# A decode-attention kernel's first weight load, issued as 16 rows and then 112

## The chip, the cores and the metric

The kernel runs on one core of a Trainium2 chip. The metric is device time in microseconds (us) of one execution, with all inputs in HBM. The median of three runs is compared.

## The reference, cut to what matters

Two independent attention blocks, A and B, each with its own inputs, are computed and joined along the last axis. Each is one decode step for 8 sequences with 32 heads of 128 and a cache of 4096 positions, in bfloat16:

```python
B, Sq, D = 8, 1, 1024
H, Sk, Dh = 32, 4096, 128
...
q = (lambda x, *d: x.transpose(*d))((x @ wq).reshape(B, Sq, H, Dh), 0, 2, 1, 3)
scores = jnp.einsum("bhqd,bhkd->bhqk", q, k_cache) * (Dh ** -0.5)
p = _softmax(scores, axis=-1)
o = jnp.einsum("bhqk,bhkd->bhqd", p, v_cache)
return (lambda x, *d: x.transpose(*d))(o, 0, 2, 1, 3).reshape(B, Sq, H * Dh) @ wo
```

The caches are 8 x 32 x 4096 x 128 each. With the four of them, the two `wq` and the two `wo`, the core reads 1107 MB in all.

## The kernel before, in words

The work is cut into 64 tiles (`NQ`), each for one sequence of one block and 8 of its heads. A tile's keys are 8 MiB in SBUF: 128 partitions of 64 KB. Partition `u*16 + m` holds head `u` and the `m`-th sixteenth of the positions. A tile's values have the same shape, and so do a `wq` and a `wo`.

All of these go through one buffer, `ring`, with three slots of 128 partitions x 64 KB. A list named `plan` fixes the order of the loads and the slot of each: `wq` of A into slot 1, the first keys into slot 0, `wq` of B into slot 2, and then keys and values in turn. `load_tiles` walks along that list. It issues a load as soon as the instruction that last reads the slot's former tenant is known, and makes the load wait for that instruction. Every load is one DMA on SyncE's queue (SP), issued at line 208 of the helper `dma`. A DMA adds 16 to a semaphore when it has landed; there is one semaphore for each slot (`("t", w)`), and `_Program` counts what each reader has to wait for.

The instructions of every engine are written into lists first (`P.add`) and then emitted. SyncE's list is emitted in two parts: its first two instructions, the loads of `wq` of A and of the first keys, stand ahead of the block in which all engines start (`part=(0, 2)`), the rest inside it (`part=(2, None)`). The repeated middle of the other engines' lists is emitted as loops whose waits grow by a fixed step.

At the start the small input `x` of both blocks is loaded on ScalarE's queue into the first 8 partitions of slot 2 (16 KB for each block). TensorE transposes it (line 447) into `xT`; then slot 2 is free for `wq` of B. `make_q` (line 285) multiplies `xT` with `wq`, `make_qT` (line 301) transposes the queries, and `make_stage` and `make_qbc` (lines 312 to 319) copy the query of a tile to all partitions that need it.

For each tile, in four chunks, VectorE multiplies the keys with the query in place (line 330) and folds the result once (line 335); TensorE sums it further through an identity (line 345), and VectorE finishes the sum (line 353). After the four chunks VectorE and ScalarE make the softmax (lines 359 to 365), VectorE spreads the weights (line 370), and TensorE multiplies them with the values (line 382). The last matmuls at line 345 free a key slot, those at line 382 a value slot. At the end `make_proj` (line 431) multiplies with `wo`, whose last load is cut into four along its columns, and two DMAs write the result.

Of the kernel before, what the change touches and what calls it, by code (L numbers as in the profile page):

```python
# [31 lines left out]
class _Program:  # L32
# [11 lines left out]
    def add(self, eng, emit, deps=(), dma_key=None, moves=False):  # L44
        op = _Op(eng, emit, list(deps), dma_key, moves)
        if dma_key is not None:
            self.counts[dma_key] = self.counts.get(dma_key, 0) + 16
            op.token = (dma_key, self.counts[dma_key])
        for d in op.deps:
            if not (d.eng == "pe" and eng == "pe"):  # L50
                d.sig = True
        self.ops[eng].append(op)
        return op
# [86 lines left out]
def _build_kernel(nc, caches, out):  # L140
    B, Sq, D = caches[0][0].shape
    _, H, Sk, Dh = caches[0][1].shape
    NC = len(caches)
    assert B == 8 and Sq == 1 and Dh == 128 and Sk == 4096 and D == 1024 and H % 8 == 0 and 128 % H == 0
    DC = D // 128
# [16 lines left out]
    with es:  # L162
# [36 lines left out]
        sems = {e: es.enter_context(nc.semaphore(f"c_{e}")) for e in ENGINES[1:]}  # L199
# [4 lines left out]
        P = _Program()  # L204
        add = P.add

        def dma(out_ap, in_ap, key, deps, eng="sp"):
            return add(eng, lambda e: e.dma_start(out_ap, in_ap), deps, dma_key=key)
# [22 lines left out]
        opT, opMul, opEacc, opRed, opNgm, opExp = {}, {}, {}, {}, {}, {}  # L231
# [18 lines left out]
        def where(n):  # L250

            return n // (B * HB), n // HB % B, n % HB
# [4 lines left out]
        def load_tiles():  # L257
            while issued[0] < len(plan):
                kind, n, w = plan[issued[0]]
                prev = before[issued[0]]  # L260
                dep = opUse.get(prev)
                if prev is not None and dep is None:
                    return
                to, key = ring[:, w, :], ("t", w)
                if kind in ("k", "v"):
                    c, b, hb = where(n)
                    from_ = caches[c][1 if kind == "k" else 2][b, hb * HQ:(hb + 1) * HQ].rearrange("u (m t) d -> (u m) (t d)", m=MP)
                    opT[(kind, n)] = dma(to, from_, key, [dep])
                elif kind == "wq":
                    opT[(kind, n)] = dma(to[:, 0:DC * H * Dh], caches[n][3].rearrange("(p k) n -> p (k n)", k=DC), key, [dep])  # L270
                else:
                    from_ = caches[n][4].rearrange("(p r) n -> p (r n)", r=H)
                    for i, (r0, r1) in enumerate(wo_cuts if n == NC - 1 else ((0, H),)):
                        opT[(kind, n, i)] = dma(to[:, r0 * D:r1 * D], from_[:, r0 * D:r1 * D], key if n < NC - 1 else ("w", i), [dep])
                issued[0] += 1
# [167 lines left out]
        def emit_xT(e):  # L443
# [5 lines left out]
            return i  # L449
        op_xT = opUse[("x", 0)] = add("pe", emit_xT, [c_ident, op_x[-1]])  # L450
        load_tiles()
        c_xT = add("dve", lambda e: e.tensor_copy(xT[:], misc_bf16[:, 0:NC * DC * B]), [op_xT])
        make_q(0)
# [5 lines left out]
        for n in range(NQ):  # L459
            P.mark(n)  # L460
            for r in range(NR):
                s = n * NR + r
                make_mul(s)
                if s >= LAG:
                    make_red(s - LAG)
                if r == LAG - 1 and n >= 1:
                    make_shift(n - 1)
                fold = make_fold(s)
                if r == LAG - 1 and n >= 1:
                    make_pm(n - 1)  # L470
                if n == 0 and r == NR - 1:
                    for c in range(1, NC):
                        make_q(c)
                        make_qT(c)
                if r == 2 and n >= 1:
                    make_pv(n - 1, 0, RG // 2)
                if r == 3 and n >= 1:
                    make_pv(n - 1, RG // 2, RG)
                    make_acc(n - 1)
                if r == 2 and n + 1 < NQ:  # L480
                    make_stage(n + 1)
                    make_qbc(n + 1)
                make_eacc(s, fold)
                load_tiles()
                if r == 3 and n >= 1:
                    make_ext(n - 1)
        P.mark(NQ)
        n = NQ - 1
# [4 lines left out]
        make_pv(n, 0, RG)  # L493
        make_acc(n)
        load_tiles()
        make_ext(n)
        make_norm(1)
# [6 lines left out]
            o.token = (("x", 0), 16 * NC)  # L504
        loops = {"pe": (1, 2, (NQ - 2) // 2), "dve": (3, 2, (NQ - 4) // 2), "act": (3, HB, (NQ - 4) // HB)}

        P.run("sp", nc.sync, sems, part=(0, 2))
        with nc.Block() as block:

            @block.sync  # L510
            def _(eng):
                P.run("sp", eng, sems, part=(2, None))

            @block.tensor
            def _(eng):
                P.run("pe", eng, sems, loops["pe"])

            @block.scalar
            def _(eng):
                P.run("act", eng, sems, loops["act"])  # L520

            @block.vector
            def _(eng):
                P.run("dve", eng, sems, loops["dve"])

            @block.gpsimd
            def _(eng):
                P.run("pool", eng, sems)
# [4 lines left out]
def bass_concat_heads__mha_block_cached__mha_block_cached__decode_kernel(  # L533
    nc, A_x, A_k_cache, A_v_cache, A_wq, A_wo, B_x, B_k_cache, B_v_cache, B_wq, B_wo, out,
):
    caches = [(A_x, A_k_cache, A_v_cache, A_wq, A_wo), (B_x, B_k_cache, B_v_cache, B_wq, B_wo)]
    _build_kernel(nc, caches, out)
# [28 lines left out]
```

## Time and profile before

| | |
|---|---|
| runs | 2563.64, 2563.65, 2563.33 us (median 2563.64) |
| profiled execution, span from the first to the last instruction | 2562.3 us; the median of the runs lies 1.3 us above it |
| busy share of the span | VectorE 85%, TensorE 44%, ScalarE 5%, GpSimd 0% |
| DMA | 1107.51 MB in 19554 packets, mean 432 GB/s |
| mean granted TensorE clock | 0.685 |

Times of a profile are microseconds from the start of its span. PE is TensorE, PEld its weight loads, DVE VectorE, ACT ScalarE, POOL GpSimd; SPq and ACTq are the queues on which SyncE and ScalarE issue DMAs. A row of a timeline is: start, duration, engine, line, operation, what is written and read, the count, and in brackets how long the engine had been idle and what ended that. A row of a window is: the stretch and its length, the busy time and the number of instructions of PE, PEld, DVE, ACT and POOL, the granted clock, the mean busy share of the 16 DMA engines, and the GB/s. A packet's bytes and time are counted in the window in which it starts, so a short window can show a share above 1.

### The profile page before, as it was taken

How to read it: one execution, taken by the hardware profiler on the slowest of the kernel's cores; microseconds unless marked ns; L12 is line 12 of the kernel's file. 1: busy time of each engine (PE TensorE's matmuls, PEld its weight loads, DVE VectorE, ACT ScalarE, POOL GpSimd, SP SyncE). 2: the span in 40 equal slices, each digit the busy share in tenths (PEclk: the TensorE clock that was granted, in tenths of full speed). 3: DMA queues.
4: the chain of work that ended last, by engine and by line, in shares of the span. 5: the costliest groups of instructions: out<-in, count | busy, mean ns of one | idle time of the engine just before them, and what ended most of it. 6: DMA issues, size and time to landing. Idle time of an engine off the chain costs nothing.

```text
span 2562.3 us, 18832 instructions
## 1 busy us (share of the span) xinstructions
PE 1115.7 (44%) x7712; PEld 396.7 (15%) x7712; DVE 2170.6 (85%) x1042; ACT 129.9 (5%) x401; POOL 2.6 (0%) x15
## 2 busy tenths in 40 slices
PE   2443443443443443444444444434444434434434
PEld 1111111111111111111111111111111111111112
DVE  3898898898898898898898888988988988988983
ACT  1100000000000000000000000000000000000000
POOL 0000000000000000000000000000000000000000
PEclk7676766767767767766666766767667666767667
DMA  9999999999999999999999999999999999999999
GB/s 425 427 438 430 437 431 436 432 436 432 435 431 437 430 438 430 435 432 435 433 431 437 431 435 433 434 433 435 433 435 433 435 433 435 433 435 433 435 433 394
DMA packets 19554, 1107.51 MB, mean 432 GB/s; under 512 B 2184, under 2 KB 2248, under 8 KB 2520
## 3 DMA queue, kind: packets, MB, share of 16 engines
q1 hardware_dynamic: 19512, 1107.34, 99.9%
q8 instruction: 7, 0.11, 0.0%
q10 hardware_dynamic: 32, 0.03, 0.0%
q14 instruction: 3, 0.02, 0.0%
HBM read 1107.33 MB, written 0.03 MB: 432 GB/s over the span
## 4 chain that ended last, share of the span: by engine, by line
DMA 52%; DVE 28%; issue 16%; PE 4%; ACT 0%; another core or an unknown queue 0%; DVEq 0%; SPq 0%
DMA ring<-in_A_k_cache_dram 25%; DMA ring<-in_B_k_cache_dram 25%; DVE ring L330 10%; DVE ring L335 10%; PE red L345 4%; DVE s_sb L353 4%; DVE PM L370 3%; DMA ring<-in_B_wo_dram 2%; DVE rmax L359 1%; DVE rtmp L360 0%; ACT PM L291 0%; DVEq L135 0%; DVE ngm L363 0%; PE o L285 0%
## 5 line engine op out<-in xcount | busy, mean ns | idle before, releaser
L330 DVE TENSOR_TENSOR ring<-ring,qbc 128x8192 bf16<-128x8192 bf16 x256 | 1131.7, 4421 | 310.9 <-DMA ring<-in_A_k_cache_dram 158.0
L345 PE MATMUL red<-ring,ident 128*128 128x512 bf16 x2048 | 780.1, 550 | 1392.7 <-DVE ring L335 1392.7
L335 DVE TENSOR_TENSOR ring<-ring 128x4096 bf16<-128x4096 bf16 x256 | 582.3, 2274 | 0.0
L345 PEld LDWEIGHTS red<-ring,ident 128*128 128x128 bf16 x2048 | 238.5, 127 | 1842.6 <-DVE ring L335 1495.2
L353 DVE TENSOR_REDUCE s_sb<-red 128x64 f32<-128x1024 f32 x256 | 312.0, 1219 | 2.9 <-PE red L345 2.9
L382 PE MATMUL pv<-ring,PM 128*32 128x512 bf16 x4096 | 274.4, 415 | 4.6 <-DVE PM L370 4.6
L370 DVE TENSOR_TENSOR PM<-pe,own_h 128x2048 bf16<-128x2048 bf16 x64 | 146.2, 2284 | 0.7 <-ACT pe L365 0.7
L382 PEld LDWEIGHTS pv<-ring,PM 128*32 128x32 bf16 x4096 | 103.9, 104 | 188.4 <-issue 116.2
L319 ACT ACTIVATE qbc<-misc 128x128 bf16<-128x128 f32 x64 | 17.8, 278 | 1093.4 <-PE misc L317 1093.4
L365 ACT ACTIVATE pe<-s_sb,ngm 128x256 bf16<-128x256 f32 x64 | 32.5, 508 | 470.2 <-DVE ngm L363 470.2
L390 ACT ACTIVATE accS<-pv 128x512 bf16<-128x512 f32 x64 | 38.2, 597 | 350.5 <-PE pv L382 350.5
L399 PEld LDWEIGHTS o<-accS,E 128*32 128x32 bf16 x1024 | 31.3, 100 | 49.3 <-issue 48.1
L399 PE MATMUL o<-accS,E 128*32 128x32 bf16 x1024 | 38.1, 185 | 0.7 <-ACT accS L390 0.7
L405 ACT ACTIVATE o_sb<-o 32x32 f32 (+1 forms) x64 | 11.9, 186 | 449.5 <-PE o L399 448.9
L359 DVE TENSOR_REDUCE rmax<-s_sb 128x1 f32<-128x256 f32 x64 | 26.9, 420 | 2.2
L435 DVE CAST orow<-proj 128x256 bf16<-128x256 f32 x2 | 0.8, 424 | 28.7 <-PE proj L431 28.7
L431 PE MATMUL proj<-ring,on_sb 128*32 128x256 bf16 x256 | 12.1, 363 | 17.7 <-DMA ring<-in_A_wo_dram 9.9
L312 ACT ACTIVATE qst<-qT 128x128 bf16 (+1 forms) x64 | 18.7, 293 | 2.0 <-DVE qT L305 2.0
L305 DVE COPY qT<-misc 128x64 bf16<-128x64 bf16 x8 | 3.5, 436 | 17.6 <-PE misc L301 17.6
L360 DVE TENSOR_SCALAR rtmp<-half,rmax 128x32 f32<-128x32 f32 x64 | 15.4, 241 | 2.2
L363 DVE TRANSPOSE_TENSOR_REDUCE ngm<-rtmp 128x1 f32<-128x32 f32 x64 | 13.5, 211 | 2.2
L317 PE MATMUL misc<-ident,qst 128*128 128x128 bf16 x64 | 14.8, 232 | 0.9 <-ACT qst L312 0.9
(33 smaller groups left out, 65.5 us busy)
## 6 DMA issues: line engine op xcount, KB each, us to landing
ring<-in_B_wo_dram SPq DMA_DIRECT2D x1, 5120.0 KB, 33.6
ring<-in_B_wo_dram SPq DMA_DIRECT2D x1, 2048.0 KB, 38.2
ring<-in_B_wo_dram SPq DMA_DIRECT2D x1, 768.0 KB, 39.6
ring<-in_A_k_cache_dram SPq DMA_DIRECT2D x32, 40.0
ring<-in_A_v_cache_dram SPq DMA_DIRECT2D x32, 27.8
ring<-in_B_k_cache_dram SPq DMA_DIRECT2D x32, 39.8
ring<-in_B_v_cache_dram SPq DMA_DIRECT2D x32, 27.8
ring<-in_B_wo_dram SPq DMA_DIRECT2D x1, 256.0 KB, 39.7
```

Of the source, the lines that this page charges most:

```text
L312: return e.activation(qst[:, n % 2, :].rearrange("p (j m) -> p j m", m=MP), from_.unsqueeze(2).to_broadcast([128, HQ, MP]), ACTF.Copy)
L319: opQbc[n] = add("act", lambda e: e.activation(qbc[:, n % 2, :], misc[:, 0:Dh], ACTF.Copy), [opQb[n], _at(opMul, NR * (n - 2) + NR - 1)])
L330: opMul[s] = add("dve", lambda e: e.tensor_tensor(v, v, qbc[:, n % 2, :].unsqueeze(1).to_broadcast([128, CT, Dh]), ALU.mult), [opT[("k", n ...
L335: return add("dve", lambda e: e.tensor_tensor(v[:, :, 0:64], v[:, :, 0:64], v[:, :, 64:128], ALU.add), [opMul[s]])
L345: i = e.matmul(dst, ident[:], v[:, g, :, j, :], start=(j == 0), stop=(j == 3))
L353: opRed[s] = add("dve", lambda e: e.tensor_reduce(s_sb[:, n % 2, r * CT:(r + 1) * CT], red_ps[s % 2][:, :].rearrange("p (t w) -> p t w", w ...
L359: m = add("dve", lambda e: e.tensor_reduce(rmax[:], s_sb[:, n % 2, :], AX.X, ALU.max), [opRed[NR * n + NR - 1]])
L365: opExp[n] = add("act", lambda e, at: e.activation(pe[:], s_sb[:, n % 2, :], ACTF.Exp, bias=ngm[:, n % 2:n % 2 + 1], scale=scale, accum_ou ...
L370: opPM[n] = add("dve", lambda e: e.tensor_tensor(PM[:], pe[:].unsqueeze(2).to_broadcast([128, T, HQ]), own_h[:].unsqueeze(1).to_broadcast( ...
L382: i = e.matmul(pv_ps[32 * q:32 * (q + 1), :], PM[:, t:t + 4, :].rearrange("p t j -> p (t j)"), v[:, t * Dh:(t + 4) * Dh], start=(g == 0), ...
L390: opAcc[n] = add("act", lambda e: e.activation(accS[:], pv_ps[:], ACTF.Copy), [opPV[n], _at(opExt, n - 1)])
L399: x = e.matmul(to, E[:, i, PH - 1 - u:PH - 1 - u + MB], accS[:, i * 128 + H * u:i * 128 + H * (u + 1)], start=(i == 0 and u == 0), stop=(i ...
```

## The change

The first load of the list, `wq` of block A, is issued as two DMAs one after the other on the same queue: the first takes partitions 0 to 15, the second partitions 16 to 127. Both add to the semaphore of slot 1, and the readers wait for both. `wq` of B stays one DMA. Since SyncE's list is one instruction longer at its head, three instead of two of its instructions are emitted ahead of the block, so the first keys' load still is. Nothing else is changed.

```diff
                 elif kind == "wq":
-                    opT[(kind, n)] = dma(to[:, 0:DC * H * Dh], caches[n][3].rearrange("(p k) n -> p (k n)", k=DC), key, [dep])
+                    from_ = caches[n][3].rearrange("(p k) n -> p (k n)", k=DC)
+                    for p0, p1 in ((0, 16), (16, 128)) if n == 0 else ((0, 128),):
+                        opT[(kind, n)] = dma(to[p0:p1, 0:DC * H * Dh], from_[p0:p1, :], key, [dep])
...
-        P.run("sp", nc.sync, sems, part=(0, 2))
+        P.run("sp", nc.sync, sems, part=(0, 3))
...
-                P.run("sp", eng, sems, part=(2, None))
+                P.run("sp", eng, sems, part=(3, None))
```

## The prediction

> **What bounds the kernel now.** I read the page's head first, then its queues, then the windows of the steady part, then the issues and the chain of the first 60 us, and last the first five microseconds in narrow windows.
>
> ```profile
> span 2562.3 us, 18832 instructions
> DMA  9999999999999999999999999999999999999999
> GB/s 425 427 438 430 437 431 436 432 436 432 435 431 437 430 438 430 435 432 435 433 431 437 431 435 433 434 433 435 433 435 433 435 433 435 433 435 433 435 433 394
> q1 hardware_dynamic: 19512, 1107.34, 99.9%
> DMA 52%; DVE 28%; issue 16%; PE 4%; ACT 0%; another core or an unknown queue 0%; DVEq 0%; SPq 0%
> ```
>
> ```profile
> 0.00:80.00 80.00, 27.35 (x241) 11.15 (x242) 33.84 (x23) 11.76 (x21) 2.60 (x15) 0.76 0.98 421
> 80.00:2480.00 2400.00, 1051.89 (x6992) 366.66 (x6990) 2096.48 (x992) 115.17 (x371) 0.00 (x0) 0.68 1.00 434
> 2480.00:2562.30 82.30, 36.44 (x482) 18.91 (x480) 40.23 (x27) 2.95 (x9) 0.00 (x0) 0.67 0.94 403
> ```
>
> The last two columns of the windows are the DMA engines' mean busy share and the GB/s. From 80 to 2480 us the sixteen engines are busy all the time (1.00) at 434 GB/s, and VectorE, the busiest compute engine, has 2096 of 2400 us. SyncE's queue q1 alone takes 99.9% of the engines' span. So the engines that move the caches set the time, and there is no idle stretch in which a delay of theirs could be made up: what the first load loses or gains comes out at the end, nearly one for one. One engine moves 434 / 16 = 27.1 GB/s, so a ring row of 64 KB costs it 2.42 us, and a whole load of 128 rows (8.39 MB) 19.3 us.
>
> ```profile
> 0.80 0.39 SPq L208 DMA_DIRECT2D ring<-in_A_wq_dram  x1
> 1.26 0.41 SPq L208 DMA_DIRECT2D ring<-in_A_k_cache_dram  x1
> 16.89 0.33 SPq L208 DMA_DIRECT2D ring<-in_B_wq_dram  x1
> 29.25 0.33 SPq L208 DMA_DIRECT2D ring<-in_A_k_cache_dram  x1
> ...
> ring<-in_A_wq_dram SPq DMA_DIRECT2D x1, 22.1
> ...
> 23.03 3.59 PE L285 MATMUL o<-ring,xT 128*8 128x512 bf16 x32 [6.17 <-DMA ring<-in_A_wq_dram]
> ...
> 34.33 0.28 ACT L319 ACTIVATE qbc<-misc 128x128 bf16<-128x128 f32 x1 [0.38 <-PE misc L317]
> ...
> 43.48 4.43 DVE L330 TENSOR_TENSOR ring<-ring,qbc 128x8192 bf16<-128x8192 bf16 x1 [9.87 <-DMA ring<-in_A_k_cache_dram]
> ```
>
> These are the starts of the DMAs on SyncE's queue and of the compute that waits for them. The load to be split is issued at 0.80 and lands 22.1 us later; the first key tile is right behind it in the same queue, and VectorE waits for that tile until 43.48. The queries' side work (23.03 to 34.6) ends 9 us before that, so what sets VectorE's start is the transfers.
>
> **The change part by part.** It splits one issue of 128 rows into one of rows 0 to 15 and one of rows 16 to 127, in the same queue and ahead of everything else. The bytes are the same; no compute instruction is changed. What the sixteen engines do at the start today is seen in narrow windows; a window counts a transfer's bytes where the transfer starts.
>
> ```profile
> 0.00:1.75 1.75, 0.00 (x0) 0.00 (x0) 0.00 (x0) 0.00 (x0) 0.86 (x8) 1.00 0.00 0
> 1.75:1.85 0.10, 0.00 (x0) 0.00 (x0) 0.00 (x0) 0.00 (x0) 0.10 (x1) 1.00 6.00 1966
> 1.85:1.95 0.10, 0.00 (x0) 0.00 (x0) 0.00 (x0) 0.00 (x0) 0.07 (x1) 1.00 9.74 3277
> 1.95:2.05 0.10, 0.00 (x0) 0.00 (x0) 0.00 (x0) 0.00 (x0) 0.06 (x1) 1.00 10.00 3277
> 2.05:2.15 0.10, 0.00 (x0) 0.00 (x0) 0.00 (x0) 0.00 (x0) 0.10 (x1) 1.00 4.03 1311
> 2.15:2.70 0.55, 0.00 (x0) 0.00 (x0) 0.38 (x3) 0.00 (x0) 0.41 (x3) 1.00 0.28 119
> 2.70:4.80 2.10, 0.00 (x0) 0.00 (x0) 0.03 (x1) 1.28 (x1) 1.01 (x5) 1.00 0.00 0
> 4.80:5.40 0.60, 0.00 (x0) 0.00 (x0) 0.00 (x0) 0.00 (x0) 0.00 (x0) 1.00 4.03 1748
> ```
>
> GB/s times microseconds gives KB: 197 + 328 + 328 + 131 + 65 = 1049 KB, which is 16 rows of 65.5 KB. Then nothing starts for 2.1 us, and between 4.80 and 5.40 the next 1049 KB start. So the undivided load already begins with a wave of 16 rows, one for each engine, of which 15 start within 0.4 us. All that is left to gain lies ahead of it.
>
> *The earlier start, a gain.* From the issue at 0.80 to the first rows (1.75 to 1.85) pass about 1.0 us, and the last engine starts in 2.15 to 2.70. If a short load came out of the queue faster, the stagger of 15 engines (0.4 us) and some of the 1.0 us could go. Bounds: 0 and 1.0 us; I take 0.2, since the SyncE issue of a full load (0.33 to 0.41 us) is the only part of that wait that can plainly depend on the number of rows. [...]
>
> *One issue more on SyncE.* 0.33 to 0.41 us by the rows above. It moves the first key load from 1.26 to about 1.7, which is needed when the engines run out of the first load, about 21 us: hidden under 19 us of transfers. The 112 rows are issued at about 1.2 and are needed at 4.80, when the first wave ends; if that cover of 3 us were gone, the 0.4 us would show. Everything further down that queue waits for compute (16.89, 29.25) and not for SyncE. The ScalarE queue's x loads share the engines row by row; if they come later, the transposes and the issue at 16.89 come later too, but the engines have the first key tile to move until about 41 us, so 24 us hide that. Cost: 0.
>
> *The wait.* Both parts count on the same semaphore and the matmuls at 23.03 wait for both; every later count on it is 16 higher. No wait instruction is added. Cost: 0.
>
> *The narrow destination, the price.* Today 16 rows are in flight at a time as well, but as parts of a transfer over all 128 rows of the ring. In the change the first wave goes to 16 neighbouring rows of SBUF. No load of the trace is like that, so I bound it. Lower end: the engines set the pace and the wave costs 2.42 us as any other, extra 0. Upper end: the write side takes a rate in proportion to the rows that a transfer spans. The row of 434 GB/s for 128 then gives 54 GB/s for 16, and 1049 KB take 19.4 us, extra 16.9. Neither end has a nearer row than the other; I take the middle, 10.9 us for the wave, extra 8.5. [...]
>
> *The 112 rows.* They make seven rows for each engine instead of eight. 128 rows are evidently dealt out so that the engines don't hinder each other (434 GB/s); 112 rows that begin at row 16 are another deal, and neighbours may share what 128 rows keep apart. Lower end: 7 x 2.42 = 16.9 us, extra 0. Upper end: the slowest engine meets another's rows at each of its seven, each costs one more row time, extra 16.9. I take two of seven, 4.8 us, nearer to the lower end because the full load, the closest in kind, shows no such loss. The slowest engine counts, since a load has landed only when its last row has, and at share 1.00 that engine has no pause in which to catch up.
>
> Sum: -0.2 + 0 + 0 + 8.5 + 4.8 = +13.1 us. The profiled execution's span of 2562.3 becomes 2575.4; the median of the three runs, 2563.64, stands 1.3 above that span, so the forecast is 2576.7 us, 0.5% slower. A measurement of this kernel can tell about 0.2%, or 5.1 us, from no change.
>
> **The rivals.** *Nothing to see.* The write side has room for sixteen engines on any rows, or rows are dealt to the engines by their address, so that the split changes no engine's list. Then only the start moves, by -1.0 to +0.4: about 2563.4 us, not slower. For it: the first wave today is 16 rows at once and the rate drops in none of the 40 slices but the last; the decisive point is whether the first wave of 16 rows ends at 4.80 to 5.40 as now. Against it: all of those loads span 128 rows, so they say nothing of 16 neighbours.
>
> *The whole first load crowded.* If the 112 rows are dealt to the engines like cards, each wave of sixteen goes to neighbouring rows, and all eight waves pay 8.5 us: +68, 2631 us. For it: a wave is one row for each engine, and if neighbouring rows go to the engines in turn in the first, they may in the other seven. Against: a full load then should suffer too, and it runs at 434 GB/s.
>
> *A faster start that carries through.* The gain's upper bound is 1.0 us, 0.04%, so it stays below what can be told; to be faster by 5.1 us the whole startup of 1.8 us would not be enough.
>
> **How the numbers follow.** Forecast (crowded first wave, some crowding behind it, from +5.1 to +19) 0.67; nothing to see 0.24; the whole load crowded 0.08; a gain over 5.1 us 0.01. So faster 0.01, same 0.24, slower 0.75. The forecast's own range is 2568.7 to 2582.6, its top being 16.9 for the first wave and a little of the second part. The range has to leave out no more than 2 in 10: with the likeliest case alone it would leave out 3, so it reaches down over "nothing to see" to 2563.0, and the wholly crowded load stays outside: 2563.0 to 2582.6.
>
> **What would show it.** In the first five microseconds the first wave of 1049 KB should start about as now, and the next rows not at 4.80 but near 13. The landing of the first load, as seen by the first L285 matmul, moves from 23.03 to about 36, the first L330 from 43.48 to about 56.6. The first slice of GB/s (a fortieth, 64 us) falls from 425 to about 425 x (64 - 13) / 64 = 338, while the DMA share stays at 9 because crowded engines count as busy; from 80 us on every slice keeps its rate, and the end lies 13 us later. The step of the narrow destination is wrong if the second wave starts by 5.4; the step of the 112 rows is wrong if the landing's delay equals the first wave's; the step of no recovery is wrong if the first L330 is late by more than the end is.

## The result, and the profile after

The changed kernel takes 2585.38 us (median of 5 runs, 2584.42 to 2585.89), the one before 2563.43 (5 runs): a ratio of 1.0085, interval 1.0074 to 1.0096, or 22.0 us more. The forecast was 2576.7, in a range up to 2582.6. The direction was right and so was the place where the time goes, the first load; the size was not.

The page of the changed kernel, its span, the 40 slices and the queue:

```profile
span 2584.6 us, 18863 instructions
DMA  9999999999999999999999999999999999999998
GB/s 288 426 435 435 428 435 436 435 429 436 434 428 436 436 434 429 437 434 428 435 436 432 432 436 433 430 435 435 431 434 435 434 430 435 435 431 434 435 434 385
q1 hardware_dynamic: 19528, 1107.34, 99.8%
```

The first slice falls from 425 to 288 GB/s, and from the second on the rate is what it was. The DMA share stays at 9 in that slice, though only two thirds of the bytes move (288 against 425 GB/s): the share counts an engine as busy while a row takes it longer, and the first 16 rows take 8.6 us each on average (5.94 x 1.45 in the second window below). The GB/s show the loss, the share hides it.

The starts of the first transfers, in windows:

```profile
0.00:1.75 1.75, 0.00 (x0) 0.00 (x0) 0.00 (x0) 0.00 (x0) 0.86 (x8) 1.00 0.00 0
1.75:3.20 1.45, 0.00 (x0) 0.00 (x0) 0.41 (x3) 0.00 (x0) 1.09 (x5) 1.00 5.94 723
3.20:10.00 6.80, 0.00 (x0) 0.00 (x0) 0.00 (x0) 1.28 (x1) 0.66 (x4) 1.00 0.06 10
10.00:11.70 1.70, 0.00 (x0) 0.00 (x0) 0.00 (x0) 0.00 (x0) 0.00 (x0) 1.00 3.08 578
11.70:22.00 10.30, 0.00 (x0) 0.00 (x0) 0.00 (x0) 0.00 (x0) 0.00 (x0) 1.00 0.79 205
22.00:45.30 23.30, 1.12 (x17) 1.09 (x18) 0.23 (x1) 0.00 (x0) 0.00 (x0) 1.00 0.98 259
45.30:80.00 34.70, 11.03 (x105) 4.14 (x105) 15.87 (x9) 5.50 (x11) 0.00 (x0) 0.66 0.99 427
```

The first wave of 16 rows (1.45 x 723 = 1048 KB) starts as before. Of the second wave, which started between 4.80 and 5.40 before, a single row (6.80 x 10 = 68 KB) starts before 10 us, and the other 15 (983 KB) between 10 and 11.7. So the first wave ran some 5.5 us longer. But the rate stays low behind it too, at 205 and 259 GB/s, until the load has landed near 45. So the first piece isn't the only slow part: 5.5 of the 22 us show in its wave, and the rest behind it, in the 112 rows.

The timeline of the changed kernel (lines are two higher than before):

```profile
0.80 0.87 SPq L208 DMA_DIRECT2D ring<-in_A_wq_dram  x2
1.71 0.43 SPq L208 DMA_DIRECT2D ring<-in_A_k_cache_dram  x1
...
30.00 1.11 PE L449 MATMUL misc<-ident,ring 8*128 8x8 bf16 x16 [30.00 <-DMA ring<-in_B_x_dram]
31.14 0.35 SPq L208 DMA_DIRECT2D ring<-in_B_wq_dram  x1
...
45.30 3.58 PE L287 MATMUL o<-ring,xT 128*8 128x512 bf16 x32 [14.19 <-DMA ring<-in_A_wq_dram]
...
65.84 4.42 DVE L332 TENSOR_TENSOR ring<-ring,qbc 128x8192 bf16<-128x8192 bf16 x1 [10.10 <-DMA ring<-in_A_k_cache_dram]
```

The first matmul on the load is 22.3 us later (23.03 before), VectorE's first multiplication 22.4 us (43.48), and the span is 22.3 us longer. Nothing is given back in the 2500 us between.

### The profile page after: what moved, and what is told of

It reads as the page before. It is cut to its first block, busy times and chain, and to the rows that moved or that the text cites. A ratio compares the mean times of both kernels' runs of the same rounds, so it can differ in the third digit from the quotient of the medians.

```text
span 2584.6 us, 18863 instructions
## 1 busy us (share of the span) xinstructions
PE 1121.7 (43%) x7712; PEld 398.3 (15%) x7712; DVE 2170.6 (84%) x1042; ACT 130.0 (5%) x401; POOL 2.6 (0%) x15
## 4 chain that ended last, share of the span: by engine, by line
DMA 51%; DVE 27%; issue 17%; PE 4%; another core or an unknown queue 1%; ACT 0%; DVEq 0%; SPq 0%
DMA ring<-in_B_k_cache_dram 25%; DMA ring<-in_A_k_cache_dram 23%; DVE ring L332 10%; DVE ring L337 10%; PE red L347 4%; DVE PM L372 3%; DVE s_sb L355 2%; DMA ring<-in_A_wq_dram 2%; DMA ring<-in_B_wo_dram 2%; DVE rmax L361 1%; DVE rtmp L362 0%; ACT PM L293 0%; PE o L287 0%; DVEq L135 0%
```

## The experiments

Four theories were held against each other. *Ports*, as the expectations call it: where the rows lie in SBUF decides. The name was the author's assumption; no run shows what lies behind the place. *Span*, the prediction's upper bound: the rate follows the number of rows that a transfer spans. *Read side*: neighbouring source rows in HBM crowd. *Issue*: the second DMA itself costs. Each run changes the one load only, and where it needs it the number of SyncE's instructions ahead of the block; only112 also fills the rows that it doesn't load, and splitB cuts the load of B in place of A's. The diffs are shortened to the loop over the pieces of the load in question. Times are medians, with the ratio and its interval; the kernel before took 2563.4 to 2563.5 us beside them.

**Cut along the columns instead of the rows (cols).**

```diff
-for p0, p1 in ((0, 16), (16, 128)): dma(to[p0:p1, 0:DC * H * Dh], from_[p0:p1, :], key, [dep])
+for c0, c1 in ((0, 4096), (4096, DC * H * Dh)): dma(to[:, c0:c1], from_[:, c0:c1], key, [dep])
```

> The first load in two DMAs again, but both of 128 rows: columns 0 to 4095 (8 KB of every row, 1 MiB as in the change) and then the other 56 KB. Four theories stand. Ports: the place of the rows in SBUF sets the rate, so nothing is lost here, 2563.4 us within 1. Span: the rate follows the number of rows that a transfer spans, so nothing is lost either. Read side: the source rows are those of before, nothing lost. Issue: a second DMA on the queue with its 16 completions is what costs; then this one is at 2585 as the change is.

Measured: 2563.35 us, ratio 1.000 (0.999 to 1.0009). Two issues, two completions and 1 MiB first cost nothing. *Issue* is out, and a first piece of 1 MiB gains nothing either.

**Eight DMAs of 16 neighbours (nb16), and of every eighth row (st8).**

```diff
+for q in range(8): dma(to[16 * q:16 * q + 16, 0:DC * H * Dh], from_[16 * q:16 * q + 16, :], key, [dep])   # nb16
+for q in range(8): dma(to[q:128:8, 0:DC * H * Dh], from_[q:128:8, :], key, [dep])                         # st8
```

> The first load in eight DMAs of 16 neighbouring rows each. Ports: each of the eight waves is like the first of the change, which lasted from 1.8 to about 10 us, 8.2 us or 5.3 to 5.8 more than a wave of before; +42 to +46, about 2607 us. [...] Span: 16.9 us more for each wave, +135, 2698. Read side: as ports. Issue: seven more issues at 22 us, +154.

> The first load in eight DMAs of 16 rows each, every eighth row (0, 8, 16, ... and so on). [...] Span: each wave spans all 128 rows, +0, 2563. Read side, if neighbouring source rows are what crowds: the source rows are eight apart, +0, 2563. Issue: +154.

Measured: 2618.64 (ratio 1.0215, 1.0198 to 1.0232) and 2584.80 (1.0083, 1.0066 to 1.01). Per wave the extra is 55.1 / 8 = 6.9 us and 21.3 / 8 = 2.66 us. A wave of 16 neighbours takes 2.42 + 6.9 = 9.3 us, 113 GB/s, and one of every eighth row 5.1 us, 206 GB/s: 3.8 and 2.1 times as long as 2.42. *Span* is out: every eighth row spans the whole buffer and still loses half the rate (206 GB/s of 434).

**The 112 rows written out as blocks of seven (blk7).**

```diff
+for p0, p1, ps in ((0, 16, 1), *((16 + i, 122 + i, 7) for i in range(7))): dma(to[p0:p1:ps, 0:DC * H * Dh], from_[p0:p1:ps, :], key, [dep])
```

> The change with its 112 rows written out as seven DMAs of 16 rows, row 16 + i + 7e for engine e. If the one DMA of 112 rows is dealt to the engines in blocks of seven neighbouring rows, this has the same waves as the change and its time: 2585.4 within 2 us, with the first matmul on the load near 45.3. If the 112 rows are dealt otherwise, the waves behind the first differ: with rows in turn they would be those of the run of 16 neighbours, and blocks written out would come out well under 2585. Issue: six more issues, far above 2600.

Measured: 2585.27 (1.0085, 1.0068 to 1.0102), the changed kernel's time to 0.1 us. The total alone proves little, since every eighth row gave 2584.8 too. The windows say more. Between 20.5 and 22 us 16 rows start in the changed kernel and in this run, in this order below, and none in the third line, which is of the halves further down:

```profile
20.50:22.00 1.50, 0.00 (x0) 0.00 (x0) 0.00 (x0) 0.00 (x0) 0.00 (x0) 1.00 2.18 699
20.50:22.00 1.50, 0.00 (x0) 0.00 (x0) 0.00 (x0) 0.00 (x0) 0.00 (x0) 1.00 2.20 709
20.50:22.00 1.50, 0.00 (x0) 0.00 (x0) 0.00 (x0) 0.00 (x0) 0.00 (x0) 1.00 0.00 0
```

So a DMA of 112 rows behaves as seven DMAs of rows 16 + i + 7e do: as if each engine had seven neighbouring rows. Had each engine every sixteenth row, all waves would be those of the run of 16 neighbours.

**Every second row of 32 (st2), and source and destination exchanged (nb_from_st8, st8_from_nb).**

```diff
+for q in range(8): rows = slice(32 * (q // 2) + q % 2, 32 * (q // 2) + 32, 2); dma(to[rows, 0:DC * H * Dh], from_[rows, :], key, [dep])   # st2
+for q in range(8): dma(to[16 * q:16 * q + 16, 0:DC * H * Dh], from_[q:128:8, :], key, [dep])                         # nb_from_st8
+for q in range(8): dma(to[q:128:8, 0:DC * H * Dh], from_[16 * q:16 * q + 16, :], key, [dep])                         # st8_from_nb
```

> The first load in eight DMAs of 16 rows each, every second row of a group of 32. [...] Span: each wave spans a quarter of the rows, 109 GB/s, 9.7 us a wave, +58, 2621, and far from the run with every eighth row. Read side: between the neighbours and every eighth row.

> Eight DMAs of 16 rows: the destination rows are 16 neighbours, the source rows every eighth (so wq of A stands in SBUF with its rows permuted, and the queries of A are other ones; the work and the bytes are the same). Ports or span: as the run of 16 neighbours in both, about 2607 or what that run gave. Read side: as the run with every eighth row in both.

> Eight DMAs of 16 rows: the destination rows are every eighth, the source rows 16 neighbours (wq of A with its rows permuted; the same work and bytes). [...] Read side: as the run of 16 neighbours in both, about 2607 or more.

Measured: 2584.99, 2618.37 and 2584.64 us (ratios 1.0084, 1.0067 to 1.0101; 1.0215, 1.0198 to 1.0232; 1.0082, 1.0065 to 1.0099). Rows spread over 32 cost what rows spread over 128 cost, against *span* again. With the source exchanged nothing moves: to 16 neighbours it is 2618.4 whatever is read, to every eighth row 2584.6. *Read side* is out for these two patterns, and the destination alone decides. For the 112 rows, whose source rows lie seven apart, the two sides were not exchanged.

**The 112 rows alone (only112).**

```diff
-for p0, p1 in ((0, 16), (16, 128)):
+for p0, p1 in ((16, 128),):
...
+c_fill = add("dve", lambda e: e.memset(ring[0:16, 1, :], 0.0))
```

> The second part alone: the first load brings rows 16 to 127 in one DMA, rows 0 to 15 are left out and filled with zeros by VectorE (1 MiB less to load, 2.4 us). It splits the loss of 22 us. By the prediction's terms the 112 rows cost 4.8 and the time is 2563.4 - 2.4 + 4.8 = 2566. By the waves of the changed kernel, where the first matmul on the load came 22.3 us later and the first wave took 5.3 to 5.8 of that, the 112 rows cost 16 to 17, and the time is about 2577 to 2578.

Measured: 2575.33 us (1.0046, 1.003 to 1.0063). Against 2563.5 - 2.4 the 112 rows cost 14.2 us, and the first 16 the remaining 7.7 of 21.9, if the two losses simply add. The expectation from the waves was 2 us too high: by this split more of the loss belongs to the first piece than the 5.5 us of its windows.

**Halves, and the same size in another place (halves, mid64).**

```diff
+for p0, p1 in ((0, 64), (64, 128)):             # halves
+for p0, p1 in ((32, 96), (0, 32), (96, 128)):   # mid64
```

> The first load as two DMAs of 64 rows, 0 to 63 and 64 to 127. [...] If it is the number of rows or of pieces that counts, it is the same as for any other cut at 64 rows.

> The same but for the place of the cut: rows 32 to 95 in one DMA, then 0 to 31, then 96 to 127. [...] If the number of rows in a DMA counts, it is no faster than the two halves, 2584.8 or above, because 32 rows are fewer still.

Measured: 2585.10 (1.0085, 1.0068 to 1.0101) and 2574.64 (1.0044, 1.0027 to 1.006). Three pieces lose half as much as two, because of where they lie. The windows of the halves, and then of mid64:

```profile
4.00:6.50 2.50, 0.00 (x0) 0.00 (x0) 0.00 (x0) 0.70 (x1) 0.13 (x2) 1.00 0.00 0
6.50:9.00 2.50, 0.00 (x0) 0.00 (x0) 0.00 (x0) 0.00 (x0) 0.00 (x0) 1.00 2.05 419
9.00:11.50 2.50, 0.00 (x0) 0.00 (x0) 0.00 (x0) 0.00 (x0) 0.00 (x0) 1.00 0.00 0
11.50:14.00 2.50, 0.00 (x0) 0.00 (x0) 0.00 (x0) 0.00 (x0) 0.00 (x0) 1.00 2.08 426
```

```profile
4.00:6.50 2.50, 0.00 (x0) 0.00 (x0) 0.00 (x0) 0.72 (x1) 0.13 (x2) 1.00 0.97 419
6.50:9.00 2.50, 0.00 (x0) 0.00 (x0) 0.00 (x0) 0.00 (x0) 0.00 (x0) 1.00 0.99 426
9.00:11.50 2.50, 0.00 (x0) 0.00 (x0) 0.00 (x0) 0.00 (x0) 0.00 (x0) 1.00 0.97 419
11.50:14.00 2.50, 0.00 (x0) 0.00 (x0) 0.00 (x0) 0.00 (x0) 0.00 (x0) 1.00 1.99 426
14.00:20.00 6.00, 0.00 (x0) 0.00 (x0) 0.00 (x0) 0.00 (x0) 0.00 (x0) 1.00 0.85 175
```

In the halves a wave of 16 rows starts in every second window of 2.5 us. In mid64 one starts in each of them, at the full rate, as long as rows 32 to 95 are loaded (64 rows, four waves); the last wave shown belongs to rows 0 to 31, and behind it the rate falls to 175.

**Four rows lower (one28).**

```diff
+for p0, p1 in ((28, 92), (0, 28), (92, 128)):
```

> Rows 28 to 91 first, then 0 to 27 and 92 to 127. [...]

Measured once, 2594.17 us; only the first 64 rows are used here. Their windows:

```profile
1.75:3.00 1.25, 0.00 (x0) 0.00 (x0) 0.41 (x3) 0.00 (x0) 0.89 (x5) 1.00 2.39 786
3.00:4.50 1.50, 0.00 (x0) 0.00 (x0) 0.00 (x0) 1.07 (x1) 0.84 (x4) 1.00 0.10 44
4.50:5.50 1.00, 0.00 (x0) 0.00 (x0) 0.00 (x0) 0.21 (x1) 0.00 (x0) 1.00 1.81 786
5.50:6.80 1.30, 0.00 (x0) 0.00 (x0) 0.00 (x0) 0.00 (x0) 0.00 (x0) 1.00 0.48 151
6.80:8.00 1.20, 0.00 (x0) 0.00 (x0) 0.00 (x0) 0.00 (x0) 0.00 (x0) 1.00 2.03 722
```

After the first wave 12 rows (786 KB) start between 4.5 and 5.5 and 13 (866 KB) between 6.8 and 8.0. In the kernel before 16 start from 4.80 to 5.80 (1049 KB) and 16 from 7.20 to 8.20 (1065 KB). So most rows of this piece come at the pace of before and a few come late: here the loss does not reach all rows of a wave. Which engines are late, and why, these windows don't show.

**The cut in the middle of the queue (splitB).**

```diff
-for p0, p1 in ((0, 16), (16, 128)) if n == 0 else ((0, 128),):
+for p0, p1 in ((0, 16), (16, 128)) if n == 1 else ((0, 128),):
```

> The change's cut (16 rows and 112) on the first load of block B in place of that of A, so in the middle of a full queue instead of at the start. If the loss is that of crowded writes and nothing gives it back, it costs the same: 21.9 more, 2585.4. If the start is what makes it costly (empty queues, engines in step), it costs less than half, under 2575.

Measured: 2586.11 (1.0089, 1.0072 to 1.0106), 22.7 us more. So it isn't the start that makes the cut costly: behind a full queue it costs as much.

No version beats the kernel before. The cut along the columns ties with it, and its 1.0 us of startup is untouched.

## Why the prediction was wrong, by its own steps

*The engines set the time and nothing is made up: right.* The load lands 22.3 us later and the span is 22.3 us longer.

*The earlier start, -0.2: not there.* The first piece's issue took 0.41 us (the line is from the chain of waits of the changed kernel), no less than the 0.39 of 128 rows, and the first bytes start in the same 0.1 us. The rows issued don't show in the length of an issue here.

```profile
0.80 0.41 SPq L208
```

*The issue, the wait and the x loads at no cost: right.* The keys' issue moved from 1.26 to 1.71 as forecast. The x loads came 14 us later (L449 at 30.00, 15.75 before), and the issue that waits for them went from 16.89 to 31.14, still well before the first key tile was in use (65.84). The cut along the columns, with the same issues and waits, cost nothing.

*The narrow destination, +8.5: about right in size, by luck.* It measured 7.7. The term was the middle between 0 and 16.9, and the upper bound rested on a rate in proportion to the rows spanned (54 GB/s), which isn't there: 16 neighbours get 113 GB/s, and every eighth row, spanning all 128, gets 206.

*The 112 rows, +4.8: this is the step that failed.* The term let the slowest engine meet another's rows at two of its seven, at one row time (2.42 us) each. They measured 14.2, by the run with them alone, which is 5.9 row times of seven. The prediction had the bounds right (0 to 16.9) and chose near the lower one because the full load, "closest in kind", shows no loss. It isn't the closest in kind. 112 rows go out as blocks of seven do (blk7), and in that deal whole waves are slow: in the run with these rows alone the 16 second rows take 4.7 us each on average (2.36 x 2.00 in the last windows below). Two halves of 64 rows lose 21.7 us, and 64 rows from 32 to 95 lose nothing. The question was how the rows are dealt and where they lie, and not how many they are. Why the deal of seven is slow no run shows, as the last section says. The prediction's own mark for this step, a landing delayed by no more than the first wave, could only have shown that the 112 rows cost nothing; it set none for a larger cost.

*The range.* Its top took 16.9 for the first piece and only 2 us more, though the bounds of the two pieces add to 33.8. Had the range also taken in the upper bound of the second piece, 2585.4 would have been inside.

*The rivals.* "Nothing to see" fell with the first wave, which ended near 10 us, where it had been 5 and the forecast 13. "The whole load crowded" gave 2631; the run that makes every wave one of neighbours has 2618.6, and the 112 rows aren't dealt like that. Of the marks in the profile, the first matmul on the load came at 45.30 and not near 36, the first slice fell to 288 and not 338, and the DMA share stayed at 9 as said.

## What to carry to other kernels

In this kernel, whose DMA engines never pause (share 1.00 from 80 to 2480 us, before and after), a slower load was paid in full at the end: the 22 us lost in the first 45 were still there at the end. Here a load over all 128 partitions could be cut along the columns for nothing; cut by partitions, its pieces are worth checking wave by wave in the first windows, because the place of the rows alone took the rate from 434 to 206 or 113 GB/s, and the DMA share doesn't show it. Fewer bytes in the first DMA gained no earlier start here, where the undivided one already begins with 16 rows (1049 KB by 2.70 us), one for each engine.

## What was not expected of the hardware

The place of a piece matters more than its size: 64 rows from 32 to 95 load at 419 to 426 GB/s in every window of 2.5 us, 64 rows from 0 to 63 in every second one only, at half of that. What it is about the place was not shown. The 112 rows stay the most open: in the run with these rows alone the windows are

```profile
1.75:3.00 1.25, 0.00 (x0) 0.00 (x0) 0.41 (x3) 0.00 (x0) 0.89 (x5) 1.00 3.44 786
3.00:6.00 3.00, 0.00 (x0) 0.00 (x0) 0.00 (x0) 1.28 (x1) 0.85 (x4) 1.00 0.09 22
6.00:8.00 2.00, 0.00 (x0) 0.00 (x0) 1.93 (x1) 0.00 (x0) 0.00 (x0) 1.00 2.36 524
8.00:10.00 2.00, 0.00 (x0) 0.00 (x0) 2.00 (x1) 0.00 (x0) 0.00 (x0) 1.00 0.00 0
10.00:12.00 2.00, 0.00 (x0) 0.00 (x0) 2.00 (x1) 0.00 (x0) 0.00 (x0) 1.00 1.77 500
...
10.50:14.00 3.50, 0.00 (x0) 0.00 (x0) 3.50 (x1) 0.00 (x0) 0.00 (x0) 1.00 1.07 304
14.00:17.00 3.00, 0.00 (x0) 0.00 (x0) 3.00 (x1) 0.00 (x0) 0.00 (x0) 1.00 1.10 350
17.00:21.00 4.00, 0.00 (x0) 0.00 (x0) 2.78 (x1) 0.00 (x0) 0.00 (x0) 1.00 1.14 266
```

All 16 second rows (1048 KB) start between 6 and 8 us, nothing starts from 8 to 10, and almost all third rows (1000 KB) start between 10 and 12: here whole waves are late, unlike one28, where 12 and 13 rows kept the pace. Where one wave of 16 rows starts in a window, its DMA share times its length is the mean time of a row. That is 4.7 us for the second rows (2.36 x 2.00), 3.7 and 3.3 for the third and fourth, and 4.6 for the fifth, against 2.4 in the kernel before (4.03 x 0.60 in the window from 4.80). So the waves of one DMA differ, at 1048 to 1064 KB each. What makes them slow, and why not equally, was not tried.
